# A fused attention and mixture-of-experts kernel: the experts' products from fp32r pairs to fp16 pairs with a scale per weight matrix

## The chip, the cores and the metric

The kernel runs on one core of one Trainium2 chip. The metric is the device time of one execution in microseconds. The core has five engines that run their own instruction lists in order and wait for each other by semaphores: TensorE (PE in the profile; PEld is its weight load), VectorE (DVE), ScalarE (ACT), GpSimd (POOL) and SyncE (SP), which here only issues DMA transfers. Work is passed through SBUF and, out of TensorE, through PSUM.

## The reference

Eight batches of eight heads of causal attention over 576 positions of 64 elements, with a learned decay; its 4608 output rows of 512 go through a top-1 mixture of eight experts. Cut to what matters:

```python
scores = q @ k.T / 8 + minimum(bias, 0)           # causal, bias = -(cum[i] - cum[j])
x = softmax(scores) @ v                           # 4608 rows of 512
logits = xn @ en.T / tau                          # rows and expert embeddings normalised
expert_idx = argmax(logits); gate_w = softmax(logits)[expert_idx]
for e in range(8):
    h = maximum(x[mask] @ w1[e], 0)               # 512 -> 1024
    out[mask] = gate_w[mask] * (h @ w2[e])        # 1024 -> 512
```

Everything is float32 at the interface. In the kernel each factor of the experts' products is split into a high and a low part, and a product is the sum of three: high times high, high times low, low times high.

## The kernel before

**Attention** fills the first part. A loop, `step(n)`, runs over the 64 heads; the step of head n computes the scores of n, the weighted sums of head n-2 into the single PSUM tile `om`, and normalises head n-3 (`norm1` to `norm3`), which reads `om`. Its two last operations on V already use the form that the change brings to the experts: `vscale` finds a power of two for a batch, and `vcp` writes V times that scale as an fp16 high part (ACT, line 280) and the fp16 rest (DVE, line 281). The weighted sums, lines 471 to 473, are fp16 and bf16 products of 73 columns. A router picks the expert of each row, and POOL scatters the rows, 580 words each, to a table in DRAM by expert (`scat`).

**The experts** follow. Each takes 640 rows (`CAP`; rarer overflow has a loop of its own, which does not run here). The rows are gathered in five tiles of 128 (`xload`), transposed on TensorE and split on ACT and DVE (`xprep`): `xH` is the high part, `xL` the rest, both fp32r. The weights come in chunks of 128 x 512 float32, 256 KB each, 16 an expert and 128 in all: `wissue` starts a transfer on SP's queue into a ring of three to five buffers, `wcv` splits a chunk, ACT copying the high part and DVE subtracting:

```python
            nc.scalar.copy(h, a)
            nc.vector.tensor_tensor(l, a, h.bitcast(F32), op=ALU.subtract)
            wissue(1)
```

`l1(m, e, lo, hi)` makes one of eight hidden tiles: 12 products per half of the columns, 24 for the 640 rows of an expert as two halves of 320, then a Relu on ACT (line 749) and the rest on DVE (line 750). Two PSUM buffers `h` take turns. `l2(e, t)` makes one of five output tiles with 24 products of 512 columns, and DVE multiplies by the gate's weight (line 763) before POOL scatters to the output. Expert 0 is done in two parts: its first 384 rows are known two batches before attention ends, and their first layer is mixed into the last steps of the head loop; its other 256 rows come after.

**The order** is written out by hand: engines run their instructions in the order of the calls. `tail(n)` holds what the experts put into the last heads' steps (k = 1 belongs to head 57), and the loop at the end of `main` the rest. What a call issues to an engine stands behind all earlier calls' instructions on that engine.

## Time and profile before

| | before |
|---|---|
| median of 3 runs | 847.13 us (846.09 to 848.7) |
| the profiled execution | 846.12 us |
| its span, first to last instruction | 844.4 us |
| mean granted TensorE clock | 0.984 |
| busy TensorE, DVE, ACT, POOL | 811.1, 506.1, 467.6, 381.4 us |
| attention's loop, by the exponentials of its heads | about 25 to 358 us |
| experts alone | from about 365 us to the end |

The page's groups name line, engine, operation, tiles, shapes and count; behind the bar stand busy time, the mean of one in ns, and the idle time of the engine ahead of the group with what ended it. A tile has the name of the buffer that it was given, so the weights' split parts appear as `qkb`, `KC` and `wv`. Rows of the timeline are start, length, engine, line, operation, tiles and how many like instructions were merged.

### The profile page before, as it was taken

The page shows a single profiled execution, that of the slowest core. Times are in us where ns is not written, and L with a number is a line of the kernel's source. Part 1 is how long each engine was busy: PE and PEld are TensorE (multiplying, and loading weights), DVE is VectorE, ACT ScalarE, POOL GpSimd, SP SyncE. Part 2 cuts the span into 40 slices and gives each one's busy share as a digit, 9 for nine tenths or more (in the row PEclk, how much of TensorE's full clock was granted, in tenths as well). Part 3 has the DMA queues.
Part 4 walks back from the last instruction along what each step waited for, and adds up shares of the span by engine and source line. Part 5 has one row for each costly group of instructions (what it writes and reads, how often), then busy time and mean ns, then how long its engine had stood idle before and what let it go on. Part 6 is the DMA issues. An engine that isn't in the chain of part 4 may idle for free. (4 is left out here: it accounts for less than half of the span.)

```text
span 844.4 us, 18980 instructions
## 1 busy us (share of the span) xinstructions
PE 811.1 (96%) x7378; PEld 748.4 (89%) x7378; DVE 506.1 (60%) x1632; ACT 467.6 (55%) x737; POOL 381.4 (45%) x361
## 2 busy tenths in 40 slices
PE   7799999999999999989999999999999999999993
PEld 3599999999999998988999898898998998988982
DVE  7667888787888788883745254264353552642410
ACT  6599989898999989631634143143242341531300
POOL 8758797979798878525221112202202111121010
PEclk9899999999999999999999999999999999999997
DMA  8977879798887877544544254153343442541100
GB/s 158 212 161 139 178 182 195 185 192 195 182 199 158 205 161 157 160 125 149 170 131 129 75 169 132 59 166 106 120 131 92 136 133 70 170 129 37 37 38 26
DMA packets 44216, 117.13 MB, mean 139 GB/s; under 512 B 6302, under 2 KB 6688, under 8 KB 43258
## 3 DMA queue, kind: packets, MB, share of 16 engines
q0 software_dynamic: 20240, 70.92, 36.0%
q1 hardware_dynamic: 23884, 44.97, 18.3%
q8 instruction: 59, 0.97, 0.5%
q14 instruction: 33, 0.27, 0.1%
HBM read 95.23 MB, written 21.49 MB: 138 GB/s over the span
## 5 line engine op out<-in xcount | busy, mean ns | idle before, releaser
L226 POOL TENSOR_TENSOR PL<-P 128x576 f16<-128x576 f32 (+2 forms) x128 | 203.6, 1697 | 24.5 <-ACT P L446 11.8
L740 PE MATMUL h<-xH,qkb 128*128 128x320 f32 (+2 forms) x1024 | 199.1, 310 | 0.3 <-DVE hq L750 0.3
L740 PEld LDWEIGHTS h<-xH,qkb 128*128 128x128 f32 x1024 | 163.1, 188 | 1.3 <-DVE hq L750 0.6
L764 POOL DMA_INDIRECT out<-Kx,xj x40 | 39.8, 996 | 193.3 <-DVE xj L70 102.7
L763 DVE TENSOR_SCALAR Kx<-pxs,xj 128x512 f32<-128x512 f32 x40 | 30.0, 751 | 146.7 <-PE pxs L758 146.7
L667 POOL DMA_INDIRECT Qx<-xs,idx x40 | 44.0, 1101 | 156.1 <-DVE xL L692 143.5
L339 DVE CUSTOM_DVE_ANT_0 junk<-s,mS 128x192 bf16<-128x192 f32 (+3 forms) x256 | 102.1, 420 | 18.5 <-PE s L331 15.0
L471 PE MATMUL om<-vh,P 128*128 128x73 f16 x960 | 110.4, 199 | 1.6 <-DVE xt L496 1.6
L473 PE MATMUL om<-vh,PL 128*128 128x73 f16 x960 | 109.7, 198 | 1.7 <-POOL PL L226 1.7
L740 PE MATMUL h<-xL,qkb 128*128 128x320 f32 (+1 forms) x480 | 110.9, 307 | 0.0
L472 PE MATMUL om<-vl,P 128*128 128x72 f16 x960 | 109.9, 197 | 0.0
L331 PE MATMUL s<-qkb 96*128 96x288 f32 (+4 forms) x384 | 96.2, 334 | 4.5 <-DMA qkb<-P 3.0
L472 PEld LDWEIGHTS <-P 128*128 128x128 bf16 x960 | 95.1, 99 | 3.4 <-issue 1.9
L473 PEld LDWEIGHTS <-PL 128*128 128x128 f16 x960 | 94.2, 98 | 1.9 <-POOL PL L226 1.9
L758 PE MATMUL pxs<-qkb,hq 128*128 128x512 f32 x360 | 95.4, 391 | 0.0
L471 PEld LDWEIGHTS <-P 128*128 128x128 bf16 x960 | 93.9, 99 | 0.3 <-issue 0.3
L740 PEld LDWEIGHTS h<-xL,qkb 128*128 128x128 f32 x480 | 81.1, 188 | 0.0
L758 PEld LDWEIGHTS pxs<-qkb,hq 128*128 128x128 f32 x360 | 67.5, 188 | 15.3
L331 PEld LDWEIGHTS s<-qkb 96*128 96x128 f32 x384 | 66.3, 198 | 10.7 <-DVE M L339 4.2
L687 ACT CAST xH<-pxm 128x512 fp32r<-128x512 f32 x34 | 19.9, 585 | 99.7 <-PE pxm L682 99.7
L446 ACT ACTIVATE P<-tb 128x1024 f32<-128x1024 f32 x64 | 65.5, 1024 | 7.3 <-PE tb L414 4.8
L443 ACT ACTIVATE P<-ta 128x576 f32<-128x576 f32 x64 | 41.4, 647 | 34.0 <-PE ta L414 32.6
(216 smaller groups left out, 1823.9 us busy)
## 6 DMA issues: line engine op xcount, KB each, us to landing
qkb<-qkh POOLq DMA_DIRECT2D x15, 1216.0 KB, 9.3
wraw<-w1h SPq DMA_DIRECT2D x41, 256.0 KB
wraw<-w2h SPq DMA_DIRECT2D x39, 256.0 KB
vT<-vtin SPq DMA_DIRECT2D x28, 320.0 KB
KC<-qkh POOLq DMA_DIRECT2D x15, 576.0 KB, 8.2
QC<-qkh POOLq DMA_DIRECT2D x15, 576.0 KB, 7.7
Qx<-w2h SPq DMA_DIRECT2D x13, 256.0 KB
Kx<-w2h SPq DMA_DIRECT2D x12, 256.0 KB
```

The lines of the kernel that those rows point to most:

```text
L226: nc.gpsimd.tensor_tensor(out, a, b_, op=ALU.subtract)
L331: nc.tensor.matmul(out, G[g]["QB"][0:96, h, 128 * i:128 * i + 128], G[g]["KB"][0:96, h, lo:hi], start=True, stop=True)
L339: nc.vector.tensor_tensor_reduce(out=jk, in0=src, in1=ms, scale=1.0, scalar=NEG, op0=ALU.add, op1=ALU.max, accum_out=MP[n // 2][:, n % 2, ...
L443: nc.scalar.activation(P32[:, 0:576].rearrange("p (a b) -> p a b", a=2), src, AF.Exp, scale=0.125)
L446: nc.scalar.activation(HD[n]["P32"][:, 576:1600], HD[n]["tb"], AF.Exp, scale=0.125)
L471: nc.tensor.matmul(out, lh, vh[:, kb], start=(kb == 0), stop=False)
L472: nc.tensor.matmul(out[:, u:u + 72], lh, vl[:, kb], start=False, stop=False)
L473: nc.tensor.matmul(out, ll, vh[:, kb], start=False, stop=(kb == j))
L667: ins = nc.gpsimd.indirect_dma_start(out=x.bitcast(I32), out_offset=None, in_=src, in_offset=bass.IndirectOffsetOnAxis(ap=X[("i", e, t)][1 ...
L740: nc.tensor.matmul(h[:, u, 0:b - a], w[:, 128 * c:128 * c + 128], x[c][:, lo + a:lo + b], start=(c == 0 and k == 0), stop=(c == 3 and k == 2))
L758: nc.tensor.matmul(y, h[:, 128 * t:128 * t + 128], w, start=(m == 0 and k == 0), stop=(m == 7 and k == 2))
L764: nc.gpsimd.indirect_dma_start(out=out, out_offset=bass.IndirectOffsetOnAxis(ap=xf[0].bitcast(U32), axis=0), in_=ys, in_offset=None, bound ...
```

## The change

The experts' factors become fp16 pairs instead of fp32r pairs. fp16 has a narrow range of exponents, so scales come with it:

- Rows: attention's output is stored with the power of two that its batch's V already has (and `XSH`) left in, and two numbers made from it are carried in spare words of each row of the table (`ws`, columns `XW+1` and `XW+2`). `xprep` picks them up with one small DVE copy, and `gate` uses them: one to scale its small constant, one to divide the weight.
- Weights: `wsq` squares each raw chunk on ACT with a sum by partition; after eight chunks DVE copies the sums to bf16. `wnorm` adds them over partitions with a TensorE product of 8 columns against ones, into a corner of `om`, and DVE makes a power of two in five small steps (six for the second layer). The conversion multiplies by it: `wcv` now begins a matrix with `wnorm`, and its two instructions take a scale read from SBUF. `l2` multiplies by the reciprocal of both layers' scales.
- A ring for raw chunks: all eight chunks of a matrix must have been squared before the first is converted. Eight first chunks go to buffers that are free at attention's end; then 14 buffers take turns (nine in `ring`, the tile that attention's `qkb2` was, three `rw`, two more). `wissue(n)` now means: up to chunk n, and after converting chunk q the list is filled to q + 15.
- fp16 tiles are half as large, so split weights have a fixed tile for each layer (`wt`), and `h`, `xH`, `xL` move within the old buffers.

The core of the diff:

```diff
+    def wsq(to):
+        while wsqd[0] < min(to, 16 * NE):
+            q = wsqd[0]
+            wsqd[0] += 1
+            m, j = q // 8, q % 8
+            nc.scalar.activation(P32J[:, 0:512], wraw[q], AF.Square, accum_out=IX["SQ"][:, m % 2, j:j + 1])
+            if j == 7:
+                nc.vector.tensor_copy(IX["SB"], IX["SQ"][:, m % 2])
+                summed.append(m)
+
+    def wnorm(m):
+        assert summed[-1] == m
+        sc, rs, pb = IX["WS"][:, m % 2:m % 2 + 1], IX["RS"][:, m:m + 1], om[:, 504:512]
+        si = sc.bitcast(I32)
+        nc.tensor.matmul(pb, onesb, IX["SB"], start=True, stop=True)
+        nc.vector.tensor_reduce(sc, pb, AX.X, ALU.add)
+        nc.vector.tensor_scalar(sc, sc, 1.0e-30, 1.0e30, op0=ALU.max, op1=ALU.min)
...
     def wcv(n):
         for _ in range(n):
...
-            nc.scalar.copy(h, a)
-            nc.vector.tensor_tensor(l, a, h.bitcast(F32), op=ALU.subtract)
-            wissue(1)
+            if j == 0:
+                wnorm(m)
+            a, s = wraw[q], IX["WS"][:, m % 2:m % 2 + 1]
+            h, l = wt(wseq[m][0], j)
+            nc.scalar.activation(h, a, AF.Copy, scale=s)
+            nc.vector.scalar_tensor_tensor(l, a, s, h, op0=ALU.mult, op1=ALU.subtract)
+            wissue(q + 15)
...
+        k = n - NH + 8
+        if k > 0:
+            wsq((0, 1, 3, 4, 7, 8, 10, 12, 14, 16, 16)[k])
+            wcv((0, 0, 0, 0, 0, 1, 2, 2, 3, 0, 2)[k])
...
         for m in range(8):
             l1(m, e, 0 if e else SPL, CAP)
+            if m < 4:
+                wsq(16 * e + 16 + (4, 6, 7, 8)[m] if e else 25 + m)
             if e > 0 and m < 4:
                 wcv(2)
...
                 if t == (1 if e else 3):
                     wcv(2)
+                wsq(16 * e + 24 + (3, 6, 8, 11, 14)[t] if e else 28 + 3 * (t - 2))
             l2(e, t)
```

In the last heads, conversions moved from the middle of a step to its end and begin later; squares came in. ACT's list for heads 60 and 61 before (lines 443 and 446 are the exponentials, 280 the copy of V, 724 the conversion):

```order
L443 ACTIVATE P_85<-ta 128x576
L724 CAST qkb_93<-wraw 128x512
L446 ACTIVATE P_85<-tb 128x1024
L280 ACTIVATE vh_107<-V,sc 128x3x144
L443 ACTIVATE P_86<-ta 128x576
L724 CAST qkb_94<-wraw 128x512
L446 ACTIVATE P_86<-tb 128x1024
L280 ACTIVATE vh_107<-V,sc 128x2x144
```

and now (452 and 455 the exponentials, 289 the copy of V, 734 a square, 761 the conversion):

```order
L452 ACTIVATE P_85<-ta 128x576
L455 ACTIVATE P_85<-tb 128x1024
L289 ACTIVATE vh_107<-V,sc 128x3x144
L734 ACTIVATE vjunk,idx<-vh_106 128x512
L734 ACTIVATE vjunk,idx<-rv 128x512 x2
L452 ACTIVATE P_86<-ta 128x576
L455 ACTIVATE P_86<-tb 128x1024
L289 ACTIVATE vh_107<-V,sc 128x2x144
L734 ACTIVATE vjunk,idx<-mS 128x512
L761 ACTIVATE wt<-rw_187,idx 128x512
```

The square of chunk 7 (from `mS`) closes the first matrix in head 61, and the first conversion stands behind it.

TensorE and DVE at the same place now, from the last weighted sum of that step to the next head's scores (line 743 is `wnorm`'s product):

```order
L482 MATMUL om<-vh_107,PL_110 128x73
L743 LDWEIGHTS onesb
L743 MATMUL om<-idx,onesb 128x8
L416 MATMUL ta<-qkb_92 128x288 x2
L420 MATMUL ta<-QC_89,KC_91 128x288 x2
```

and DVE from V's rest to the ranks (589 to 601) and the normalisation that frees `om` (493 to 505):

```order
L290 SCALAR_TENSOR_TENSOR vl<-V,sc,vh_107 128x2x144
L736 CAST idx<-idx 128x8
L744 TENSOR_REDUCE idx<-om 128x1
L745 TENSOR_SCALAR idx<-idx 128x1
L746 TENSOR_SCALAR idx<-idx 128x1
L747 TENSOR_SCALAR idx<-idx 128x1
L748 TENSOR_SCALAR idx<-idx 128x1
L762 SCALAR_TENSOR_TENSOR wt<-rw_187,idx,wt 128x512
L589 TENSOR_TENSOR om<-om,base 128x40
L591 TENSOR_TENSOR base<-base,om 128x8
```

Before, the rows of 736 to 762 were not there: DVE's conversion for that head stood ahead of V's rest.

The third place is ACT in the second half of expert 0, hidden tiles 2 to 4. Before (749 the Relu, 683 and 687 a row tile's square and copy, 93 the gate):

```order
L749 ACTIVATE hq<-h 128x256
L683 ACTIVATE vjunk,xj<-Qx 128x512
L687 CAST xH<-pxm 128x4x128
L93 ACTIVATE xj<-xj 128x16
L749 ACTIVATE QC_89<-h 128x256
L683 ACTIVATE vjunk,xj<-Qx 128x512
L687 CAST xH<-pxs 128x4x128
L749 ACTIVATE hq<-h 128x256
L724 CAST qkb_93<-wraw 128x512 x2
```

and now (783, 696 and 700, 94):

```order
L783 ACTIVATE hq<-h 128x256
L734 ACTIVATE vjunk,idx<-ring 128x512
L696 ACTIVATE vjunk,xj<-Qx 128x512
L700 CAST xH<-pxm 128x4x128
L94 ACTIVATE idx<-xj 128x16
L783 ACTIVATE hp<-h 128x256
L734 ACTIVATE vjunk,idx<-ring 128x512
L696 ACTIVATE vjunk,xj<-Qx 128x512
L700 CAST xH<-pxs 128x4x128
L783 ACTIVATE hq<-h 128x256
L761 ACTIVATE wt<-ring,idx 128x512
L761 ACTIVATE wt<-rw_187,idx 128x512
```

A square stands behind the Relus of tiles 0 to 3; the conversions that follow tile 4 stayed where they were.

More of the change, by code (lines that the diff above doesn't have):

```diff
@@ L70, in esum, with gate @@
     nc.vector.tensor_reduce(L, e, AX.XY, ALU.add)
-def gate(nc, r, E, L, ss, g, itau, tiny):
+def gate(nc, r, E, L, ss, g, itau, tiny, ep, rx):
     n = ss.shape[1]
@@ L260, in vscale @@
         si = sc.bitcast(I32)
+        ws = p2.tile([128, 2], F32, name="ws", bufs=3)
         first.append(partial(nc.vector.tensor_reduce, sc, pb, AX.X, ALU.add))
@@ L626, in main, with wt @@
     NTL = CAP // 128
-    def cut(t, k):
-        t = t[:, 1024 * k:1024 * k + 1024]
-        return t, (t[:, 0:512], t[:, 512:1024])
-    kc = KCs[1].rearrange("p h s -> p (h s)")
-    WT[1] = [(cut(qkbs[1 + i // 2], 2 * (i % 2)), cut(qkbs[1 + i // 2], 2 * (i % 2) + 1)) for i in range(4)]
-    WT[2] = [(cut(kc, 0), cut(kc, 1))] + [(cut(qkbs[0], 2 * i), cut(qkbs[0], 2 * i + 1)) for i in range(2)]
+    def wt(kind, k):
+        if kind not in WT:
+            WT[kind] = const.tile([128, 2 * (QW + KW)], F16, tag=f"qkb{2 - kind}", name="wt")
+        t = WT[kind][:, 1024 * k:1024 * k + 1024]
+        return t[:, 0:512], t[:, 512:1024]
+    RW = [const.tile([128, 512], F32, name=f"rw{i}") for i in range(3)]
     def htile(m):
@@ L700, in main @@
     wseq = [(1, 0)] + [x for e in range(NE) for x in ((2, e), (1, e + 1))][:-1]
-    wseq = [(k, e, i, u) for k, e in wseq for i in range(4) for u in range(2)]
-    wraw = []
+    wraw, wdone, wsqd, summed = [], [0], [0], []
     def wissue(n):
-        for _ in range(n):
-            if len(wraw) < len(wseq):
-                kind, e, i, k = wseq[len(wraw)]
-                if "Kx" in HT and len(wraw) % 5 > 2:
-                    a = (HT["Kx"][:, 3], HT["Qx"][:, 3 * XR:])[len(wraw) % 5 - 3]
-                else:
-                    a = p2.tile([128, 512], F32, tag="rw", name="wraw", bufs=3)
-                nc.sync.dma_start(a, (w1h if kind == 1 else w2h)[e, i, :, 512 * k:512 * k + 512])
-                wraw.append(a)
+        while len(wraw) < min(n, 16 * NE):
+            q = len(wraw)
+            if q < 8:
+                if q == 3:
+                    RW.append(p2.tile([128, 1440], F32, tag="vl", name="rv"))
+                a = RW[q] if q < 3 else vhs[0].rearrange("p j q c -> p (j q c)").bitcast(F32)[:, 512 * (q - 3):512 * (q - 2)] if q < 5 else RW[3][:, 512 * (q - 5):512 * (q - 4)] if q < 7 else mS[:, 0:512]
+            else:
+                i = (q - 8) % 14
+                if q == 8:
+                    HT["ring"] = const.tile([128, 9 * 512], F32, tag="qkb2", name="ring")
+                a = HT["ring"][:, 512 * i:512 * i + 512] if i < 9 else RW[i - 9] if i < 12 else (HT["Kx"][:, 3], HT["Qx"][:, 3 * XR:])[i - 12]
+            kind, e = wseq[q // 8]
+            nc.sync.dma_start(a, (w1h if kind == 1 else w2h)[e, q % 8 // 2, :, 512 * (q % 2):512 * (q % 2) + 512])
+            wraw.append(a)
@@ L715, in wcv @@
     def wcv(n):
         for _ in range(n):
-            kind, e, i, k = wseq[wdone[0]]
-            a = wraw[wdone[0]]
+            q = wdone[0]
+            m, j = q // 8, q % 8
             wdone[0] += 1
-            if kind == 2 and i == 3 and len(WT[2]) == 3:
-                vt = [p2.tile([128, 1280], F32R, tag="vl", name="wv") for _ in range(2)]
-                WT[2].append((cut(vt[0], 0), cut(vt[1], 0)))
-            h, l = (w[1][k] for w in WT[kind][i])
-            nc.scalar.copy(h, a)
@@ L725, in wcv @@
-            nc.vector.tensor_tensor(l, a, h.bitcast(F32), op=ALU.subtract)
-            wissue(1)
-    wdone = [0]
+            if j == 0:
[5 more added lines that the diff above has]
+            wissue(q + 15)
     def l1(m, e, lo, hi, mid=None):
-        wH, wL = (w[1][m % 2] for w in WT[1][m // 2])
-        xH, xL = ([X[(n, e)][:, c] for c in range(4)] if n == "H" else [X[(n, e)][c // 2][:, c % 2] for c in range(4)] if e + lo + 0 == 0 and hi == SPL
-                  else [X[(n, e)][1][:, c] for c in range(4)] for n in "HL")
+        wH, wL = wt(1, m)
@@ L734, in l1 @@
+        xH, xL = X[("H", e)], X[("L", e)] if e == 0 and hi == SPL else X[("L", e)][1]
         h = ps_t.tile([128, 2, 512], F32, tag="t", name="h")
@@ L754, in l2 @@
         for m in range(8):
-            wH, wL = (w[1][m % 2] for w in WT[2][m // 2])
+            wH, wL = wt(2, m)
             hH, hL = htile(m)
@@ L1002, in main @@
         xload(0, t)
+    wsq(19)
     l2(0, 0)
+    wsq(22)
     l2(0, 1)
+    wsq(24)
     def second():
@@ L1096, in overflow @@
         esum(nc, L, x.unsqueeze(1))
-        for f in gate(nc, new([128, 4, 1], F32, "ogr"), new([128, 1, NE], F32, "ogE"), L, ss, gw, itau, tiny):
+        for f in gate(nc, new([128, 4, 1], F32, "ogr"), new([128, 1, NE], F32, "ogE"), L, ss, gw, itau, tiny, ex[:, 0:1], ex[:, 1:2]):
             f()
```

87 lines of the change are left out of this document (50 added, 37 removed).

## The prediction

> **What bounds the kernel now.** I read the page's first parts, then the table of busy time by stretches of 20 us, then TensorE's own timeline, because a busy TensorE is not yet one at its best rate. The profiled execution took 846.12 us, 1.7 us more than its span, and lies 1.0 us under the median of the runs shown (847.13). All times below, up to the last step, are inside that span.
>
> ```profile
> span 844.4 us, 18980 instructions
> PE 811.1 (96%) x7378; PEld 748.4 (89%) x7378; DVE 506.1 (60%) x1632; ACT 467.6 (55%) x737; POOL 381.4 (45%) x361
> ```
> ```profile
> 320.00:340.00 20.00, 18.50 (x277) 17.85 (x276) 18.28 (x59) 16.19 (x21) 14.60 (x14) 1.00 0.75 163
> 340.00:360.00 20.00, 18.93 (x288) 18.49 (x287) 16.57 (x44) 14.37 (x26) 12.68 (x12) 1.00 0.57 183
> 360.00:380.00 20.00, 17.69 (x171) 16.88 (x170) 17.34 (x33) 7.06 (x14) 5.49 (x6) 0.91 0.38 117
> ...
> 400.00:420.00 20.00, 19.65 (x140) 18.28 (x140) 14.32 (x42) 12.49 (x33) 5.06 (x5) 1.00 0.59 168
> ...
> 660.00:680.00 20.00, 20.00 (x138) 20.00 (x138) 12.15 (x28) 9.95 (x20) 3.21 (x4) 1.00 0.55 168
> 780.00:800.00 20.00, 20.00 (x139) 20.00 (x138) 10.62 (x25) 7.45 (x13) 0.00 (x0) 1.00 0.14 41
> ```
> The columns are the stretch, its length, then busy time of PE, weight loads, DVE, ACT and POOL, the granted clock, the DMA share and GB/s. In the last three rows, and so from 380 us to the last tiles, TensorE is idle for a third of a microsecond in all, at a granted clock of 1.00; DVE and ACT have between a quarter and two thirds of their time free. So the experts' stage is TensorE's own stream, and only its cadence counts. Between 320 and 380 us, where attention runs out, TensorE is idle 5 us in 60 and DVE is busy 52 of 60: there an added wait can show.
>
> The duration of a matmul in the groups (308 ns at 320 columns) overlaps with the next. The cadence is read from starts:
>
> ```profile
> 423.36 1.53 PE L758 MATMUL pxs<-qkb,hq 128*128 128x512 f32 x6
> ...
> 426.12 0.46 PE L740 MATMUL h<-xH,qkb 128*128 128x320 f32 x2
> 426.42 0.45 PE L740 MATMUL h<-xL,qkb 128*128 128x320 f32 x2
> ...
> 431.70 0.45 PE L740 MATMUL h<-xL,qkb 128*128 128x320 f32 x2
> ```
> From 423.36 to 426.12 there are 12 second-layer products of 512 columns: 2.76/12 = 230 ns each. From 426.42 to 431.70 there are 36 first-layer products of 320 columns: 5.28/36 = 146.7 ns each. Both are fp32r.
>
> **What fp16 does to the cadence.** Two kinds of fp16 matmul are in this trace: the warming products at its start, and attention's weighted sums, the first and the last of one head's 45.
>
> ```profile
> 4.92 4.70 PE L186 MATMUL om<-PL 128*128 128x512 f16 x21
> ```
> ```profile
> L186 PEld LDWEIGHTS <-PL x19: 98/98/98, 5.1 to 9.0; 128*128 128x128 f16 x19
> ```
> ```profile
> 342.00 0.20 PE L471 MATMUL om<-vh,P 128*128 128x73 f16 x1
> ...
> 343.47 0.20 PE L473 MATMUL om<-vh,PL 128*128 128x73 f16 x1
> ```
> The 21 warming products last 4.70 us, each alone 0.38 us, so 4.32/20 = 216 ns at 512 columns, with a weight load between each two. The 44 steps from 342.00 to 343.47 are 33.4 ns each at 73 columns, again with a load each; loads of this type are thus hidden even there. The line through both points has a slope of 182.6/439 = 0.416 ns a column and gives 33.4 + 247 x 0.416 = 136 ns at 320 columns. So fp16 saves 14 ns at 512 columns and 10.7 ns at 320.
>
> Counts, from the code: the first layer has 8 experts x 8 tiles x 24 = 1536 products (1344 of 320 columns, the rest of 256 and 384, which I take with the same saving), the second 8 x 5 x 24 = 960. Saved: 1536 x 10.7 = 16.4 us and 960 x 14 = 13.4 us, together **29.8 us**. The bound above is 35 us, if all 2496 products gained the 14 ns of the longest; the bound below is 0, if the difference were not the type's. Against 0 speaks that the fp32r cadence is the same where DMA share is 0.55 (138 products in 20 us) and 0.14 (139): it is not traffic that stretches it. I stay at 29.8.
>
> One thing weakens the first of these rows: line 148 sets the warming products' operands to zero, and one weight tile serves all 30. Attention's rows are on real data, with a new weight tile each, in stretches whose granted clock is 1.00; I give the doubt a rival below.
>
> **What is added, and who hides it.** Each of 128 raw chunks is now squared on ACT, and the conversion gets a scale read per partition.
>
> ```profile
> L724 ACT CAST qkb<-wraw 128x512 fp32r<-128x512 f32 x60 | 35.3, 617 | 0.0
> L280 ACT ACTIVATE vh<-V,sc 128x432 f16<-128x432 f32 x32 | 19.9, 621 | 0.0
> L780 DVE TENSOR_SCALAR sc<-sc 128x1 int32<-128x1 int32 x16 | 2.5, 154 | 0.5
> ```
> ```profile
> 405.56 0.62 ACT L683 ACTIVATE vjunk<-Qx 128x512 bf16<-128x512 f32 x1
> 406.08 0.19 ACT L683 ACTIVATION_READ_ACCUMULATOR vjunk<-Qx 128x1 f32 x1
> 406.18 0.58 ACT L687 CAST xH<-pxm 128x512 fp32r<-128x512 f32 x1
> 406.64 0.23 ACT L93 ACTIVATE xj<-xj 128x16 f32<-128x16 f32 x1
> ...
> 409.03 0.38 ACT L749 ACTIVATE hq<-h 128x256 fp32r<-128x256 f32 x1 [0.40 <-PE h L740]
> 409.31 1.13 ACT L724 CAST qkb<-wraw 128x512 fp32r<-128x512 f32 x2
> ```
> The timeline shows a square of 512 columns, of a row tile, and what follows: it takes 0.81 us alone and 0.62 where the next instruction starts behind it (405.56 to 406.18). 128 of them are 79 to 104 us of ACT. A scaled conversion of 512 columns is near 690 ns (621 at 432 columns with a scale by partition), 70 ns over today's 617: 9 us. DVE gets some seven tiny instructions a matrix and one a row tile, 16 x 7 x 0.15 + 40 x 0.15 = 23 us, and its 128 subtractions keep their length, as L281, the same form on PSUM, is near them. Cover: in one expert's span of TensorE (192 x 136 + 120 x 216 ns + 2 us of transposes = 54 us) ACT has 16 squares (10 to 13 us) more beside the 20 us or so that the stretches above show, and the squares stand mostly between second-layer tiles, of 5.2 us each, where ACT has a row tile's square and copy to do, 1.1 us. If that cover were gone it would cost its length, up to 14 us an expert; I take 0 for the seven later experts. TensorE's 16 sums of the squares have 8 columns each: under 1 us.
>
> Chunks must also be there in time. The order gives a chunk's square, in the worst case, three second-layer tiles (16 us) after its transfer is issued; loads of like size land in
>
> ```profile
> qkb<-qkh POOLq DMA_DIRECT2D x2, 288.0 KB, 7.0
> ```
> 7.0 us on another queue. So no wait there: 0, and the rival below prices it.
>
> Two places do lie on the path.
>
> *The first scale, in the loop of head 61.* The sum of the squares stands on TensorE ahead of head 62's scores and waits for the square of chunk 7 on ACT, behind the exponential and the copy of V, and for a DVE copy. Today's rows there, by engine:
>
> ```profile
> 345.23 0.37 PE L414 MATMUL tb<-trim,identb 128*128 128x192 bf16 x2
> ...
> 347.78 0.50 PE L407 MATMUL ta<-qkb 128*128 128x288 f32 x2
> ...
> 350.44 0.20 PE L471 MATMUL om<-vh,P 128*128 128x73 f16 x1
> ```
> ```profile
> 345.69 1.03 ACT L446 ACTIVATE P<-tb 128x1024 f32<-128x1024 f32 x1
> 346.61 0.50 ACT L280 ACTIVATE vh<-V,sc 128x288 f16<-128x288 f32 x1
> ```
> ```profile
> 347.14 0.52 DVE L281 SCALAR_TENSOR_TENSOR vl<-V,sc,vh 128x288 f16<-128x288 f32 x1 [0.79 <-ACT vh L280]
> ...
> 347.99 0.21 DVE L579 TENSOR_TENSOR om<-om,base 128x40 f32<-128x40 f32 x1 [0.32 <-PE om L473]
> ...
> 349.26 0.53 DVE L496 TENSOR_TENSOR xt<-om,z 128x360 f32<-128x360 f32 x1
> ```
> ACT is done with V's copy near 347.0, with the square near 347.75, DVE with its copy near 348.0; TensorE, ready at 347.78, sums at about 348.1 and has waited 0.4 us. Then DVE does five dependent steps of 0.15 us (349.1), ACT converts (349.7), DVE subtracts (350.4), and only then come the ranks and the normalisation, 1.8 us in today's rows (347.99 to 349.79). That frees `om`, the single tile of the weighted sums, at 352.2. TensorE wants it at 350.44 today: 1.7 us more. Together **2.1 us**; below: 0, if the 5 us of idle time around it swallow this, above: 8 us, if the delay returns in each of the four heads that follow. I take one, since DVE's list gets shorter from then on.
>
> *The second half of expert 0.* Here a first-layer tile has 256 columns, by the line above 12 x 109 ns = 1.3 us, and for it ACT has a Relu (0.3 in the rows above, 409.03 to 409.31), now for four tiles a square (0.62), for three a row tile's square and copy (1.1, 405.56 to 406.64), for three two conversions. Today's trace has its longest wait of the stage here:
>
> ```profile
> 412.02 0.28 PE L740 MATMUL h<-xH,qkb 128*128 128x256 f32 x1
> 412.65 0.39 PE L740 MATMUL h<-xH,qkb 128*128 128x256 f32 x1 [0.35 <-DVE hq L750]
> ```
> Those starts are 0.63 us apart instead of 0.12. ACT's list up to the Relu of tile 5, from the first tile's end at 1.4 us: six Relus 1.8, four squares 2.5, three row tiles 3.2, two conversions 1.2 with a wait for their scale of 1.0, the gate's small functions 0.7: it ends at 11.8, and DVE's half of the tile at 12.2. Tile 7 needs that buffer; TensorE alone would be there after seven tiles and three times 0.4 us of transposes, at 10.5. So 1.8 us of waiting where today has 0.5; with some idle time of ACT between its waits I take 2.0 us more; between 0 and 4.
>
> What runs in attention (two tiny DVE steps and a small POOL copy a batch, four more tiny transfers on SP's queue at head 0) stands beside a TensorE that is busy all the time: 0.5 us.
>
> **Sum**: 844.4 - 29.8 + 2.1 + 2.0 + 0.5 = 819.2 us of span, 820.9 us for that execution, and 822 for a median, 1.0 us higher as today.
>
> **Rivals.**
> *Attention's end costs nothing and waits inside the second layer go too.* Then 844.4 - 31 = 813 of span, 816 in all. For it: idle time is there today. Against: an in-order wait on TensorE for ACT.
>
> *ACT sets the pace of the first layer.* Relus stand in one queue behind conversions that wait for a scale (TensorE to DVE, five steps, to ACT: about 1 us) and squares. Two buffers of `h` give each Relu 3.3 us less its own 0.7 and DVE's 0.8. If each of the 15 later matrices loses 1 us, the time is 837. Against: the tiles with a new scale have no or two squares in the order.
>
> *The cadence does not move*: fp16 on data in the middle of all other traffic runs at 230 and 147 ns. Then only the 5 us of additions stay: 852, slower. For it: the 216 ns come from a quiet stretch with one weight tile. Against: the two DMA shares above, and 33 ns at 73 columns in the busiest stretch.
>
> *A late chunk stops ACT* (slower than before): the place is the last second-layer tile, where ACT squares the chunk issued three tiles ago; behind it stands the copy that the next expert needs. From a landing of about 16 us on, each further microsecond is lost in each of seven experts; it undoes the gain at 16 + 25/7 = 20 us. At 25 us of landing: 822 + 7 x 9 = 885. The row above has 7.0 us.
>
> *Products overlap more than the warming rows show*, and only the weight loads pace them, 98 ns each. Then the second layer saves 960 x 132 ns and the first 1536 x 48 ns, 201 us: 645. Against: the 216 ns row has a load between each two products. [...]
>
> **How the numbers follow.** Forecast 822 with 0.63, its own range 817 to 828; nothing lost 0.13; ACT's pace 0.14; no change of cadence 0.05; late chunk 0.03; overlap 0.01; the last 0.01 is none of these, somewhere between. For 8 in 10 the range takes in the second and most of the third: 814 to 834. Faster by over 0.3% (what a measurement of this kernel can tell from no change): the forecast, the second, third and overlap cases and the last, 0.92. The cadence and chunk cases hold 0.08; in 0.03 of it a part of the gain comes and just pays for the waits, so 0.05 is slower.
>
> **What would show it.** Starts of second-layer products 216 ns apart and of first-layer ones 136 ns (230 and 147 would refute the main term); expert spans of 54 us with TensorE idle under 0.5 us in each; a TensorE wait of about half a microsecond on DVE at the first sum of squares and one of 1 to 2 us for `om` behind it; about 2.5 us of waits in the second half of expert 0; ACT about 60% busy beside it. Idle TensorE in every first layer, with Relus behind squares, would give the third case; ACT waiting for a DMA in front of a square, the late chunk.

## The result, and the profile after

The changed kernel takes 834.71 us (median of 4 runs, 832.95 to 835.98) against 847.35 for the kernel before in the same session: a ratio of 0.985 (95% interval 0.982 to 0.987). It is faster by 12.6 us where 25.3 were forecast; the time lies 0.7 us above the predicted range.

The page of the profiled execution (834.01 us) begins:

```profile
span 832.2 us, 19540 instructions
PE 785.3 (94%) x7394; PEld 591.6 (71%) x7394; DVE 532.3 (64%) x1798; ACT 567.8 (68%) x993; POOL 377.9 (45%) x369
```

The busy time by stretches of 20 us, with the same columns as in the prediction:

```profile
340.00:360.00 20.00, 16.65 (x252) 16.12 (x249) 14.87 (x41) 13.54 (x28) 12.20 (x11) 1.00 0.65 215
360.00:380.00 20.00, 13.91 (x184) 9.89 (x183) 14.72 (x31) 12.49 (x29) 5.30 (x7) 0.91 0.23 83
...
420.00:440.00 20.00, 16.93 (x90) 9.69 (x90) 12.47 (x33) 13.54 (x32) 1.02 (x1) 0.91 0.44 134
...
660.00:680.00 20.00, 20.00 (x151) 14.41 (x150) 16.54 (x43) 13.29 (x25) 2.75 (x3) 1.00 0.59 176
```

and of before, one row that the prediction does not have:

```profile
420.00:440.00 20.00, 20.00 (x125) 18.89 (x124) 10.10 (x23) 6.33 (x13) 5.08 (x5) 1.00 0.43 132
```

At 660 us TensorE is busy throughout and does 151 products where it did 138. Between 340 and 380 us it is idle 9.4 us in 40 (3.4 before), and at 420 us, where it had no gap, 3.1 in 20. So the gain is in the experts, and it is lost where attention ends and in expert 0. Starts of heads' exponentials and of first products cut the two profiles into stages; the prediction's terms are shared out among these by their counts of products:

| stage | before, us | after, us | change | predicted |
|---|---|---|---|---|
| start to head 56's exponential | 319.4 | 320.0 | +0.6 | +0.5 |
| head 56 to the first second-layer product | 63.8 | 72.4 | +8.6 | +2.1 - 1.0 |
| from there to expert 1 | 42.9 | 46.4 | +3.5 | +2.0 - 2.7 |
| expert 1 | 58.1 | 55.7 | -2.4 | -3.7 |
| experts 2 to 7, to the end | 360.2 | 337.8 | -22.4 | -22.4 |

The cadence is what was forecast. TensorE in expert 2, first layer and second layer:

```profile
503.74 0.44 PE L774 MATMUL h<-xL,wt 128*128 128x320 f16 x2
...
508.63 0.43 PE L774 MATMUL h<-xL,wt 128*128 128x320 f16 x2
```
```profile
521.04 0.81 PE L792 MATMUL pxs<-wt,hv 128*128 128x512 f16 x3
...
523.63 1.46 PE L792 MATMUL pxs<-wt,hq 128*128 128x512 f16 x6
```

36 products of 320 columns in 4.89 us are 136 ns each, 12 of 512 in 2.59 us are 216.

What TensorE waited for between 336 and 400 us (total, times, longest):

```profile
PE om L480 <- DVE xt L505: 4.5, 3, 1.7
PE h L774 <- DVE wt L702: 3.4, 1, 3.4
PE om L743 <- DVE idx L736: 2.1, 1, 2.1
```

Two of these three come from tiny DVE instructions that took microseconds, each beside POOL. DVE, then POOL, in that stretch:

```profile
348.87 2.24 DVE L736 CAST idx<-idx 128x8 bf16<-128x8 f32 x1
...
361.10 4.04 DVE L691 SCALAR_TENSOR_TENSOR xj<-Qx,idx 128x1 int32<-128x1 int32 x1
```
```profile
349.03 2.04 POOL L232 TENSOR_TENSOR PL<-P 128x576 f16<-128x576 f32 x2
...
361.09 4.03 POOL L232 TENSOR_TENSOR PL<-P 128x576 f16<-128x576 f32 x4
```

The first is the copy of the sums, 8 columns; the second reads one number a row. Elsewhere in this profile the first line takes 0.16 to 0.17 us (0.43 twice) and the second 0.14 to 0.16. Each ends when POOL's subtractions end (351.11 and 365.14 us, POOL's at 351.07 and 365.12). On ACT, the first conversion of head 61, and then expert 0's second half:

```profile
352.12 0.72 ACT L761 ACTIVATE wt<-rw,idx 128x512 f16<-128x512 f32 x1 [3.29 <-DVE idx L747]
```
```profile
418.49 0.39 ACT L783 ACTIVATE hq<-h 128x256 f16<-128x256 f32 x1
421.01 0.72 ACT L761 ACTIVATE wt<-ring,idx 128x512 f16<-128x512 f32 x1 [2.14 <-DVE idx L747]
...
423.33 0.38 ACT L783 ACTIVATE hq<-h 128x256 f16<-128x256 f32 x1
```
```profile
424.54 0.27 PE L774 MATMUL h<-xH,wt 128*128 128x256 f16 x1 [2.67 <-DVE hq L784]
```

ACT stands at a conversion until its scale is there. Behind it in ACT's list are a second conversion, a row tile and the Relu of tile 5 (423.33), and TensorE waits for that tile.

### The profile page after: what moved, and what is told of

Same layout as the page of the kernel before. It is cut to its first block, busy times and chain, and to the rows that moved or that the text cites. A ratio compares the mean times of both kernels' runs of the same rounds, so it can differ in the third digit from the quotient of the medians.

```text
span 832.2 us, 19540 instructions
## 1 busy us (share of the span) xinstructions
PE 785.3 (94%) x7394; PEld 591.6 (71%) x7394; DVE 532.3 (64%) x1798; ACT 567.8 (68%) x993; POOL 377.9 (45%) x369
## 5 line engine op out<-in xcount | busy, mean ns | idle before, releaser
L774 PEld LDWEIGHTS <-wt 128*128 128x128 f16 x1536 | 149.4, 98 | 70.3 <-issue 12.3
L774 PE MATMUL h<-xH,wt 128*128 128x320 f16 (+2 forms) x1024 | 189.6, 301 | 6.4 <-DVE hq L784 4.8
L797 DVE TENSOR_SCALAR Kx<-pxs,xj,idx 128x512 f32<-128x512 f32 x40 | 32.4, 810 | 124.8 <-PE pxs L792 124.8
L679 POOL DMA_INDIRECT Qx<-xs,idx x40 | 41.1, 1028 | 145.3 <-DVE xL L702 129.1
L774 PE MATMUL h<-xL,wt 128*128 128x320 f16 (+1 forms) x480 | 106.4, 298 | 0.0
L792 PE MATMUL pxs<-wt,hp 128*128 128x512 f16 x360 | 97.6, 380 | 0.0
L792 PE MATMUL pxs<-wt,hq 128*128 128x512 f16 x360 | 90.8, 380 | 0.0
L792 PEld LDWEIGHTS <-hp 128*128 128x128 f16 x360 | 35.4, 98 | 42.9 <-issue 0.8
L792 PEld LDWEIGHTS <-hq 128*128 128x128 f16 x360 | 35.2, 98 | 42.2
L792 PE MATMUL pxs<-wt,hv 128*128 128x512 f16 x240 | 64.6, 383 | 0.0
```

The lines of the kernel that those rows point to most:

```text
L679: ins = nc.gpsimd.indirect_dma_start(out=x.bitcast(I32), out_offset=None, in_=src, in_offset=bass.IndirectOffsetOnAxis(ap=X[("i", e, t)][1 ...
L774: nc.tensor.matmul(h[:, u, 0:b - a], w[:, 128 * c:128 * c + 128], x[:, c, lo + a:lo + b], start=(c == 0 and k == 0), stop=(c == 3 and k == 2))
L792: nc.tensor.matmul(y, h[:, 128 * t:128 * t + 128], w, start=(m == 0 and k == 0), stop=(m == 7 and k == 2))
L797: nc.vector.tensor_scalar(ys, y, xf[3], IX["RS"][:, 2 * e + 1:2 * e + 2], op0=ALU.mult, op1=ALU.mult)
```

## Experiments

Thirteen kernels and the change a second time, all timed against the kernel before. There is one profile of each; the stages in the table at the end are read from it. Of each edit its core is shown.

**What is the price of the scales?** Constant scales, nothing computed:

```diff
+        rs2 = IX["RS"].rearrange("p (e k) -> p e k", k=2)
+        for ap, x in ((IX["WS"][:, 0:1], 4.0), (IX["WS"][:, 1:2], 2048.0), (rs2[:, :, 0], 0.25), (rs2[:, :, 1], 2.0 ** -13)):
+            nc.gpsimd.memset(ap, x)
...
     def wsq(to):
+        return
...
-            if j == 0:
-                wnorm(m)
```

> The weight scales are constants, set once (the powers of two that the computed ones come to for these inputs); the 128 squares, the 16 copies, sums and their DVE steps are left out. The conversions keep their scale operand, the ring and the fp16 halves stay. Theory A (the lost 12 us are the price of the computed scales: squares, sums and what waits behind them): 844.4 - 29.8 + 0.5 of span, 816 to 819 as a median, and TensorE's idle time from 337 us on back near the 8.4 us of before. Theory B (a faster TensorE finds the waits of attention's end and of expert 0 anyway, because ACT's and DVE's conversions and row work set the pace there): 826 to 833, with waits of several us left between 340 and 425 us.

826.26 us (824.11 to 833.06; ratio 0.977, 0.973 to 0.981). So squares, sums and their waits cost 8.4 us, not all of the loss: from head 56 to the second layer this kernel still takes 69.6 us, 5.8 more than before. The time lies in theory B's range (826 to 833) and not in theory A's (816 to 819), though most of what theory A put on the scales did come back. DVE and POOL in the stretch:

```profile
351.57 2.65 DVE L764 SCALAR_TENSOR_TENSOR wt<-rw,idx,wt 128x512 f16<-128x512 f32 x1
354.15 0.19 DVE L592 TENSOR_TENSOR om<-om,base 128x40 f32<-128x40 f32 x1
```
```profile
351.62 2.05 POOL L235 TENSOR_TENSOR PL<-P 128x576 f16<-128x576 f32 x2
```

A conversion, at the end of a step now, stands beside POOL's subtractions and takes 2.65 us where it takes 0.75 elsewhere, and the ranks (line 592 on) wait behind it.

Only the first matrix constant:

```diff
+        nc.gpsimd.memset(IX["WS"][:, 0:1], 4.0)
+        nc.gpsimd.memset(IX["RS"][:, 0:1], 0.25)
...
+            if m == 0:
+                continue
             nc.scalar.activation(P32J[:, 0:512], wraw[q], AF.Square, accum_out=IX["SQ"][:, m % 2, j:j + 1])
...
-            if j == 0:
+            if j == 0 and m:
                 wnorm(m)
```

> Only the first matrix (W1 of expert 0) has a constant scale: its 8 squares, its copy, its sum in the loop of head 61 and the five DVE steps are left out, everything else is as in the change. Theory A: the waits at 348.87 (2.25 us) and 353.79 (1.5 us) go, and with them the late start of the first layer; if the delay is merely carried, the end moves by 3 to 4 us (830 to 832); if it also caused the waits behind it in the first layer's tiles (+9 us at the first second-layer product), by 7 to 9 us (826 to 828). Theory B: at most 1 us, because the next wait takes its place.

835.57 us (0.986, 0.984 to 0.988): no gain, as theory B has it. Head 60 to 63 takes 15.5 us instead of 16.4, but TensorE then waits 3.9 us at the row tiles' transposes; from head 56 to the second layer it is 74.0 us. The next wait took the place of the first.

The copy dropped, fp32 sums:

```diff
-                nc.vector.tensor_copy(IX["SB"], IX["SQ"][:, m % 2])
...
-        nc.tensor.matmul(pb, onesb, IX["SB"], start=True, stop=True)
+        nc.tensor.matmul(pb, ones, IX["SQ"][:, m % 2], start=True, stop=True)
```

> The bf16 copy of the sums of squares on DVE is dropped in all 16 matrices; TensorE multiplies the fp32 sums by fp32 ones instead. If the copy at 348.87 lasted 2.24 us only because POOL held what DVE needs (its two subtractions run from 349.03 to 351.07, and the copy ends when they do), the wait ahead of the first sum falls from 2.1 us to under 0.3, and the time by 2 us or a little more (832 to 833). If the sum was late because of ACT's squares, the wait stays near 2 us and the time at 834.7.

The wait for the first sum is gone, as the collision has it; the time is not: 835.53 us (0.987, 0.985 to 0.989). TensorE's waits from 336 to 400 us:

```profile
PE pxs L695 <- DVE wt L702: 4.6, 1, 4.6
PE om L480 <- DVE xt L505: 4.4, 4, 1.4
```

Where the change waited 3.4 us at a first-layer tile and 1.0 at a row tile, this kernel waits 4.6 at a row tile. All waits that the view lists come to 12.0 us here and to 14.1 in the change, and the stretch is 71.3 us, 1.1 less than in the first profile of the change. The whole did not get shorter, in part because the fp32 sum has a price of its own, which my expectation left out: it runs as two products, 0.39 us where the change's sum takes 0.17, and experts 2 to 7 take 339.5 us where the change takes 337.8.

```profile
350.62 0.39 PE L742 MATMUL om<-idx,ones 128*128 128x8 f32 x2
```

So neither edit made the kernel faster, but this one does not show that the wait at the first sum was worth nothing.

**Expert 0's second half.** The squares of chunks 19 to 27 earlier:

```diff
-    wsq(19)
+    wsq(21)
     l2(0, 0)
-    wsq(22)
+    wsq(25)
     l2(0, 1)
-    wsq(24)
+    wsq(28)
```

> The squares of chunks 19 to 27 stand two to four earlier in ACT's list, so that none is left among the first four first-layer tiles of expert 0's second half. If squares make the Relus late there, the waits of 1.1 and 2.8 us at 419 and 421.6 us fall to under 1 us together, the stretch at half clock behind them goes too, and the time falls by 3 to 5 us (830 to 832). If DVE or the row tiles set the pace there, the waits stay and the time is 834 to 835.

838.11 us (0.990, 0.988 to 0.991), above both ranges that I gave, but not for this edit: its profile is 3.9 us later at head 56, where the code is the same, and 2.0 us longer from there to the second layer, where it is the same too. In the half itself 1.9 us came off (26.8 us from its first product to expert 1, 28.7 in the first profile of the change); the wait of 2.67 us on TensorE stayed. Then the scale ahead as well:

```diff
-            if j == 0:
+            if j == 0 and m != 2:
                 wnorm(m)
...
     wsq(28)
+    wnorm(2)
```

> The change with the squares of chunks 19 to 27 earlier (as in the run of that name), and the sum and scale of the third matrix computed ahead of the third second-layer tile of expert 0, no longer in front of its first conversion. Theory D: what stops expert 0's second half is ACT, which waits 2.1 us in order for that scale behind DVE's list, with the Relu of tile 5 behind it. Then the wait of 2.8 us on TensorE falls below 1 us, and the stretch from the first first-layer product of that half to expert 1 takes 24 to 25 us (28.8 in the change, 26.9 with the squares earlier, 25.3 before). If conversions and row tiles alone fill ACT there: 26.5 or more.

25.4 us for the half, just above the 24 to 25 that I gave, and 833.61 us (0.984, 0.982 to 0.986). ACT goes from the Relu to the conversions without a wait, the wait of 2.67 us on TensorE is 0.46, and the clock stays:

```profile
420.62 0.41 ACT L783 ACTIVATE hq<-h 128x256 f16<-128x256 f32 x1
420.89 0.75 ACT L761 ACTIVATE wt<-ring,idx 128x512 f16<-128x512 f32 x1
```
```profile
416.00:436.00 20.00, 18.29 (x125) 12.19 (x123) 15.37 (x48) 16.54 (x42) 3.92 (x4) 1.00 0.54 175
```

Theory D is shown for this place: 1.4 us were the scale that its conversions stood waiting for. The squares are worth 1.2 to 1.6 us and not 1.9: the first profile of the change has 3.4 us at half clock in this half, and in two profiles with the same order and none it takes 28.0 (the second of the change) and 28.4 us (the run with the first matrix constant).

Squares without sums, by constant scales with `wsq` left in place and its copy dropped:

> The 128 squares are done as in the change, but the scales are the constants: no copy, no sum on TensorE, no five DVE steps, and no conversion waits for a scale. Constant scales without squares took 826.3, the change 834.7. If the in-order waits for the scales cost the 8.4 us between them: 826 to 828, expert 0's second half 25 to 26 us. If ACT's time for the squares does: 833 to 835. By the two runs on that half (1.9 us came off with earlier squares, 1.5 with an earlier scale) I expect it between: 829 to 831.

830.93 us (0.982, 0.977 to 0.988), as expected: of the 8.4 us about half are the squares, half the sums and the waits for them. The halves are rough, since the four runs of this kernel and of the one with constant scales spread over 7 and 9 us.

**The conversions' places.** With constant scales, expert 0's 16 conversions back where the kernel before has them:

```diff
...
-            wissue(q + 15)
+            if "ring" in HT:
+                wissue(q + 15)
...
-            wcv((0, 0, 0, 0, 0, 1, 2, 2, 3, 0, 2)[k])
...
     def tail(n):
         k = n - NH + 8
+        if 1 <= k < 9:
+            wcv(1)
...
             l1(k - 8, 0, 0, SPL)
+            if k > 8:
+                wcv(2)
...
-        if m < 5 or m == 7:
+        if m < 5:
             wcv(2)
```

> Constant scales as in the run before (no squares, no sums), and the 16 conversions of expert 0 stand where the kernel before has them: one in each of the heads 57 to 64, then two behind each of the next four first-layer tiles, where the change has none up to head 60 and 1, 2, 2 and 3 in the four heads behind. From the exponential of head 56 to the first second-layer product the kernel before took 63.9 us, the change 72.3, constant scales 69.6. Theory C (the conversions were pushed together into the four heads where DVE and ACT are needed most, and that costs the 5 to 7 us which constant scales left): 62 to 65 us in that stretch, 819 to 822 as a median. If the loss comes from elsewhere (the transfers of the ring, the collisions of DVE with POOL): 68 us or more, 825 to 827.

821.75 us (0.969, 0.967 to 0.971), 64.1 us from head 56 to the second layer. Theory C is shown: the places cost 4.5 us by the medians, 5.5 in that stretch (3.5 by the next run). What moved is the instruction that is held. DVE and POOL in this kernel:

```profile
368.16 2.70 DVE L465 TENSOR_TENSOR PL<-P 128x576 f16<-128x576 f32 x1
```
```profile
366.20 4.03 POOL L235 TENSOR_TENSOR PL<-P 128x576 f16<-128x576 f32 x4
```

Beside POOL's four subtractions DVE stands here too, 2.70 us for an instruction of 0.75, but the row tiles are done and it is DVE's own half of the same subtraction that stands still, for which nobody waits yet. So it is in the next run and in the last one below, which have the same places, and so it was before the change (the row of 4.97 us, below).

The ring filled a chunk or two at a time:

```diff
-                wissue(q + 15)
+                wissue(q + 7)
...
-            wissue(16)
+            wissue(10)
```

> As the run with constant scales and conversions at their places of before; and the ring is not filled by nine transfers at once near 342 us (2.4 MB, behind which the row gathers issued at 345 us landed only from 349 us on), but a chunk or two at a time, seven ahead of the conversion. If that burst of transfers delays rows, scatters or code, the stretch from head 56 to the second layer is 2 us or more shorter than with the burst (another 2 to 3 us off the time). If it is hidden anyway: the same within 1 us.

821.19 us (0.970, 0.968 to 0.972): the same time. The stretch from head 56 to the second layer did not get shorter; it took 66.1 us in this profile, 2.0 more than with the burst, which is neither of the two that I expected. So the burst costs nothing that these runs show.

**Other orders of the whole change.** The sum a head earlier:

```diff
-            wsq((0, 1, 3, 4, 7, 8, 10, 12, 14, 16, 16)[k])
-            wcv((0, 0, 0, 0, 0, 1, 2, 2, 3, 0, 2)[k])
+            wsq((0, 1, 3, 5, 8, 8, 10, 12, 14, 16, 16)[k])
+            wcv((0, 0, 0, 0, 0, 1, 2, 2, 1, 1, 1)[k])
...
         if k == 5:
+            wnorm(0)
...
-        if m < 5 or m == 7:
+        if m in (3, 4, 6, 7):
             wcv(2)
```

> The change with the eight squares of the first matrix done one head earlier, its sum in front of head 61's weighted sums instead of behind that head's square, and three of the last conversions moved from head 64 into the first layer's tiles. If the in-order waits for that scale (2.25 us on TensorE, 3.3 us on ACT) set the length of attention's end, the stretch from head 56 to the second layer falls from 72.3 us to 67 to 69 (828 to 831). If they only stand beside other waits (DVE held by POOL, conversions in few heads): 71 to 74, and 833 to 836.

838.99 us (0.989, 0.987 to 0.991), above both ranges that I gave, and 73.8 us: no gain. Squares in heads 57 to 59, sum in head 60, conversions from there on:

```diff
+            wsq((0, 2, 5, 8, 8, 9, 10, 12, 14, 16, 16)[k])
+            wcv((0, 0, 0, 0, 1, 1, 1, 2, 1, 1, 1)[k])
...
         if k == 4:
+            wnorm(0)
...
+        if k == 10:
+            wnorm(1)
...
```

> The whole change, with computed scales, but in another order: seven raw chunks of the first matrix are loaded at head 56 (four of them into the places of the converted weights that are written later), its squares are done in heads 57 to 59, its sum stands in head 60, its conversions come one a head from there (two in head 63) and one behind each of the first layer's first tiles; the sum of the second matrix stands ahead of the third tile, without a conversion behind it; the third matrix' scale is computed ahead of expert 0's second half as in the run before. Theories C and D together (conversions in few heads, and conversions right behind a sum, cost the 12 us): from head 56 to the second layer 65 to 68 us (72.3 in the change, 64.0 with constant scales at the places of before), expert 0's second half 25 to 26 us, 824 to 829 as a median. If squares and sums themselves cost the time wherever they stand: 831 to 836.

838.98 us (0.989, 0.985 to 0.992) and 77.7 us to the second layer: no better than the change, and theories C and D together, as I had put them, fell. Half of the expectation held, expert 0's second half took 25.0 us. Both orders with the ring filled two chunks a head:

> As the run with the third matrix' scale computed ahead (833.6), but the ring is filled two chunks a head and not nine at once near 342 us. Theory E: what makes the stretch of the last heads long and different from run to run (16.4 and 20.8 us from head 60 to 63 in two profiles of the change, 20.6 in that run) is traffic: the row gathers, the scatters and TensorE's own code stand behind 2.4 MB of chunks. Then that stretch takes 14 to 17 us and the time 827 to 830. If it is ACT and DVE alone: 20 us and 832 to 835.

> As the run in the other order (839.0), with the ring filled two chunks a head. Theory E: 828 to 832, and the stretch from head 60 to 63 falls from 21.2 to 17 us or less. Without it: 837 to 840.

835.35 us (0.986, 0.982 to 0.990) and 839.83 (0.989, 0.984 to 0.994), heads 60 to 63 in 20.7 and 21.4 us. Theory E, that nine chunks issued at once make the stretch long, is out.

So I took the work out of the last heads without leaving any out. Expert 0's chunks are loaded a second time, squared in 16 heads in mid attention, summed there:

```diff
+    PRE = [8 * b + c for b in (1, 2, 3, 4, 5) for c in (6, 7, 8, 9)][:16]
+    def wpre(n):
...
+        if n in PRE:
+            i = PRE.index(n)
+            issue(i + 2)
+            nc.scalar.activation(P32J[:, 0:512], RW[i % 3], AF.Square, accum_out=IX["SQ"][:, i // 8, i % 8:i % 8 + 1])
+        for m in range(2):
+            if n == PRE[8 * m + 7] + 2:
+                summed.append(m)
+                wnorm(m)
...
```

> The scales of expert 0's two matrices are computed in the middle of attention: their 16 chunks are loaded once more, one in each of 16 heads between head 14 and 41 that have no square of a value tile, squared on ACT there, summed two heads behind the last of eight. With the scales at hand the conversions stand where the kernel before has them (one in each of heads 57 to 64, then two behind each of four tiles), and heads 57 to 64 have no square and no sum. The third matrix' scale is ahead of expert 0's second half, as in the run of that name. If squares, sums and conversions close together in the last heads are what costs there: from head 56 to the second layer 64 to 67 us as with constant scales at those places, 823 to 827 in all. Against it: ACT is busy 18.3 of 20 us in mid attention, and 4 MB more are loaded there; if these are not hidden, heads 14 to 42 get longer by up to 16 x 0.75 = 12 us, and the time is 828 to 838.

828.18 us (826.53 to 831.01; ratio 0.979, 0.976 to 0.982): faster than before and, by 6.5 us, than the change, with all scales computed; 5.4 us faster than the run with the third scale ahead, whose edit it takes in. It is 1.2 us above the range expected. Head 56 to the second layer takes 63.5 us, from there to expert 1 40.7. Mid attention pays: from head 8 to head 56 it is 247.5 us (244.2 before), of which the two sums are this, between 170 and 275 us:

```profile
PE om L743 <- DVE om L565: 1.5, 2, 0.7
```

**Chance.** The change a second time:

> The change itself once more, for the spread of its stages between two profiles. In six kernels that have the same code up to head 56, that head's exponential came between 318.2 and 324.0 us, and two kernels with the same code up to the second layer took 72.3 and 74.4 us from there. If this is chance of a run, the stages here differ from those of the first profile (320.0 and 72.3) by as much; if it belongs to a build, they are the same within 0.5 us.

837.95 us, a single run; 323.5 us to head 56, 74.8 us from there, 3.5 and 2.4 us more than in the first profile. So such differences do not belong to the program. Whether each execution draws them anew is not shown: the four runs with the squares earlier (836.4 to 839.5 us) all lie above the four of the change. Differences of 3 us between whole kernels say little here, and the stages behind are what to read: experts 2 to 7 take 337.6 to 338.3 us in 14 of the 15 profiles of changed kernels, 339.5 in the one with fp32 sums.

Part of this chance can be read. The table also gives how long TensorE's granted clock was at a half between head 56 and the second layer (all times in us).

| kernel | median, us | head 56 to second layer | at half clock in it | to expert 1 |
|---|---|---|---|---|
| before | 847.4 | 63.8 | 3.4 | 42.9 |
| the change, first and second profile | 834.7, 838.0 (one run) | 72.4, 74.8 | 3.4, 10.2 | 46.4, 44.4 |
| fp32 sums | 835.5 | 71.3 | 6.8 | 47.5 |
| squares only, constant scales | 830.9 | 70.4 | 6.8 | 44.4 |
| constant scales | 826.3 | 69.6 | 6.8 | 42.4 |
| the same, conversions at the old places | 821.8 | 64.1 | 0 | 41.1 |
| the same, ring filled little by little | 821.2 | 66.1 | 3.4 | 41.0 |
| third scale ahead | 833.6 | 74.2 | 6.8 | 43.2 |
| first sum and squares earlier, spread | 839.0 | 77.7 | 13.7 | 46.2 |
| first two scales in mid attention | 828.2 | 63.5 | 0 | 40.7 |

At half clock a second-layer product takes 0.43 us (three from 427.07 to 428.35 in the first profile of the change) where it takes 0.216 at the full one, so a stretch at half clock costs at most half its length. Taken off at this most, an estimate, it leaves 70.7 and 69.7 us for the two profiles of the change, 70.8 with the third scale ahead and 70.9 for the spread order: the difference between these kernels can be the clock alone. Constant scales come to 66.2, with the conversions at the old places to 64.1 and 64.4. So without the clock 2.1 us are left for the conversions' places, of 5.5, and 3.5 to 4.5 us between the change and constant scales.

## Why the prediction was right or wrong

**The cadence term, -29.8, was right** and came from rows of other parts of the trace: 216 ns and 136 ns were forecast from 21 warming products and 45 sums of one head, and both are there to the nanosecond. Experts 2 to 7 gained 22.4 us, as forecast. The case that the cadence does not move, the case of overlap at 98 ns a load, and the case of ACT setting the pace of later first layers fall with these rows. The late chunk did not come either: where a square waited for a transfer at all, it was this much in eight:

```profile
L734 ACT ACTIVATE vjunk<-Kx 128x512 bf16<-128x512 f32 x8 | 5.0, 630 | 0.7 <-DMA Kx<-w1h 0.6
```

**The first scale, +2.1, was mis-sized**: the stretch lost 9.6 us against the cadence, 7.5 more than the term. Even its upper bound of 8 us, "if the delay returns in each of the four heads that follow", was too low. The half clock is no part of this, for the profiles of before and after both have 3.4 us of it there. Two steps failed.
- The conversions' new places were costed at nothing. The order shown ahead of the prediction has them leave the middle of a step for its end and eight heads for four; with constant scales this alone costs 4.5 us by the medians and 3.5 to 5.5 in the stretch (69.6 against 66.1 and 64.1 us), part of it by time at half clock (6.8 us of it against 3.4 and 0). The sum counted what was added and did not price what was moved.
- Each DVE step was taken at its own length, 0.15 us for a tiny one. The trace of before had the counterexample, one instruction of 0.75 us that took 4.97:

```profile
360.48 4.97 DVE L453 TENSOR_TENSOR PL<-P 128x576 f16<-128x576 f32 x1
```
```profile
360.80 4.03 POOL L226 TENSOR_TENSOR PL<-P 128x576 f16<-128x576 f32 x4
```

Beside it POOL ran four subtractions. DVE was held there for over 4 us, and TensorE did not wait for the held instruction: its two waits beside it, of 1.14 and 0.51 us, end at POOL. A list that comes a microsecond later puts another one there: the copy for the sum, then the first number of a row tile, ahead of the low part that the first layer needs. The wait at the first sum was forecast at 0.4 us and was 2.1; the one for `om` behind it at 1.7, and was 1.3.

Without the first matrix' squares and sum the stretch took 74.0 us, without the copies 71.3, and with the same work in other orders 73.8 to 77.9, against 72.4 and 74.8 in the two profiles of the change. All squares and sums left out brought 69.6, and these out and the conversions at the old places 63.5 to 66.1. So squares and sums together with the conversions' new places are shown to be what the last heads do not hide. What squares and sums would cost with the conversions at the old places no run tells. Which of the waits between 345 and 370 us would be the last one is open too: the second profile of the change lacks the held instruction of 361.10 and is not shorter.

**Expert 0's second half, +2.0, was mis-sized** by 4.2 us with the right mechanism: ACT's list makes the Relu of tile 5 late and tile 7 waits, 2.67 us. The list that was added up counts the two conversions at 1.2 us, where the prediction's own price of 690 ns makes it 1.4; that is little. Their wait for their scale was put at 1.0 us and is 2.1, because DVE has the gate's last steps (419.23 to 420.01 us) ahead of the scale's five (420.26 to 421.16); and the squares, taken as time on a list, cost 1.2 to 1.6 us that could stand elsewhere. The half clock behind the gap, for which the sum had no term, adds to it: 3.4 us of it (0.91 over 20 us), so at most 1.7.

**Expert 1 was counted among the seven that cost nothing**; it lost 1.3 us of its gain, and with constant scales it has it back (54.2 us).

The case that nothing is lost comes true, within 2 us a stage, for constant scales at the old places from head 56 on (64.1, 41.1 and 54.2 us, where the cadence alone gives 62.8, 40.2 and 54.4); its 821.8 us still lie above the 816 of that case, since that profile reached head 56 4.6 us later than before. That the forecast of 822 is the time of that kernel is luck: it has none of the scales that the terms were for.

## What to carry to other kernels

When a change moves work, price each moved instruction at its new place, by what runs beside it there, as carefully as the added ones. In a group of equal instructions look at the longest one, not only at the mean: one that takes six times its length (here 4.97 us for 0.75, beside POOL's 4.03) makes one ask what will stand in that spot once the lists shift. And do not put a conversion straight behind the reduction that makes its scale (here 1.4 us in expert 0's second half); where a stretch is already full, move such a reduction to a stretch that has the engine to spare, even at the price of loading its input twice (here 828.18 us against 833.61).

## What of the hardware was unexpected

- Some DVE instructions stood still beside POOL's `tensor_tensor` from and to SBUF: an 8-column copy for 2.24 us, a one-column instruction for 4.04, subtractions and conversions of 0.68 to 0.75 us for 1.6 to 5.0, in the profiles of this case. In the rows above DVE is held until POOL is done: the copy and the one-column instruction end 0.04 and 0.02 us after POOL's last subtraction, the longer ones 0.55 to 0.63 us after it. Four subtractions in a row held one DVE instruction through their 4.03 us. To start first did not help: by the recorded starts DVE was first by 0.16 us at 348.87 in the change and by 0.32 at 360.48 before, and was held all the same; POOL was then at the end of an indirect DMA, whose row stops at 349.00 and at 360.78. Why these instructions are held is not shown.
- The same wait came with a lower clock in one profile and not in another. The wait of 2.67 us in expert 0's second half is in both profiles of the change; in the first the granted clock of the stretch behind it is 0.91, in the second it is this, 1.00:

```profile
430.19 0.27 PE L774 MATMUL h<-xH,wt 128*128 128x256 f16 x1 [2.67 <-DVE hq L784]
```
```profile
423.00:443.00 20.00, 16.10 (x98) 9.65 (x98) 13.26 (x41) 14.92 (x37) 2.37 (x3) 1.00 0.48 149
```

  Up to the last products the half clock comes in pieces of 3.41 us and multiples (one each from 367.41 and 425.44 us in the first profile), and within a profile their starts are whole multiples of 3.41 us apart (those two 58.03 us, 17 times 3.41). Cut at these points, the waits of the first and then of the second profile fall like this (the half clock follows in the first):

```profile
422.02:425.44 3.42, 0.90 (x9) 0.81 (x9) 3.42 (x9) 3.18 (x8) 0.00 (x0) 1.00 0.51 146
425.44:428.85 3.41, 3.41 (x15) 2.07 (x13) 2.49 (x6) 2.39 (x6) 0.00 (x0) 0.50 0.55 166
```
```profile
425.91:429.33 3.42, 1.47 (x12) 1.17 (x12) 2.68 (x12) 2.66 (x7) 0.00 (x0) 1.00 0.41 93
429.33:432.74 3.41, 2.55 (x20) 2.00 (x20) 2.90 (x7) 2.57 (x7) 0.00 (x0) 1.00 0.66 223
```

  TensorE is idle for 2.5 us of one piece in the first profile, for 1.9 and 0.9 us of two in the second; that this makes the difference is a guess. Over all 16 profiles, from 300 to 800 us, half clock followed each of the 27 such pieces with 1.98 us or more of idle TensorE, and of those that were at full clock themselves 5 of the 21 with 1.6 to 1.98 and one of the 2256 with less.
- Up to head 56 kernels with the same code differed by up to 6 us (318.2 to 324.0), most of it between the exponentials of heads 1 and 2 (9.6 us in the change, 14.0 with constant scales at the old places). It goes with the half clock there: it lasts 10.2 us in the eight profiles where the two are 9.6 to 10.1 us apart, and 13.7 or 17.1 in the eight where they are 11.1 to 15.1 apart.
- In several profiles TensorE has small waits in the last heads that nothing in the trace ends. In the second profile of the change:

```profile
363.52 0.24 PE L423 MATMUL tb<-trim,identb 128*128 128x192 bf16 x1 [0.53 <-issue]
364.23 0.27 PE L423 MATMUL tb<-trim,identb 128*128 128x256 bf16 x1 [0.46 <-issue]
```

  Heads 60 to 63 took 19.9 to 21.4 us in the seven profiles with computed scales that have them, and 16.4 in the first profile of the change, which has none. But three profiles with constant scales have them too and took 13.6 to 14.4, and the second profile of the change has 4.2 us at half clock in these heads. So it is not shown that they make the stretch long. With the transfers spread they stayed, so nine chunks issued at once are not their cause; it is open.
